# A gated linear recurrence and a spatial gating unit in one kernel: from scheduled batches to a hand-ordered pipeline of chunks

## The chip, the cores and the metric

The kernel runs on one core of a Trainium2 chip. The metric is device time in microseconds (us). A core has TensorE (PE in the profile; PEld is its weight loading), VectorE (DVE), ScalarE (ACT), GpSimd (POOL) and SyncE (SP), which take their instructions in order, each from its own queue, and signal each other by semaphores. Sixteen DMA engines move data between HBM and SBUF; TensorE writes into the eight banks of PSUM.

## The reference

Batch 4, 8 heads, sequence 768, head dimension 48; model width 384, d_ff 1024. The inputs and the output are float32.

```python
# part 1, for every batch and head
for t in range(S):
    state = alpha[t][:, None] * state + outer(k[t], v[t])
    y[t] = q[t] @ state
# part 2, x is y as (batch, seq, heads * dim)
h = relu(x @ w_in);  u, v = h[..., :512], h[..., 512:]
v_n = (v - mean(v)) / sqrt(var(v) + 1e-6)          # over the last axis
v_s = einsum('ts,bsd->btd', w_spatial, v_n) + b_spatial[None, :, None]
out = (u * v_s) @ w_out
```

## The kernel before

Part 1 cuts the sequence of a batch into six chunks of 128 steps, with all eight heads of a chunk side by side (128 partitions, 384 columns). `part1_front` loads q, k and v with a cast to bf16 from GpSimd's queue (L137 to L139) and alpha in float32 from SP's (L140); takes the logarithm of alpha (`la`, L143), sums it along time with a matmul by a triangle of ones (`cum_ps`, L146), and takes both exponentials (L151, L152). q is multiplied by the one on VectorE (`qt`, L158), k by the other on GpSimd (`kt`, L159). Sixteen small matmuls give each head's k^T v and its total decay (L164, L170), from which the state is carried on (L175 to L183: ScalarE, VectorE, GpSimd, ScalarE). q and k are transposed on TensorE (L190, L191), copied into `qkT` by VectorE for the even heads (L193) and by ScalarE for the odd ones (L194), and multiplied head by head (L202); VectorE applies the causal mask (`ptm`, L209). `part1_back` adds the part inside the chunk and the part from the state (L222, L228), and transposes y into `xT_b` (L237 to L242).

Part 2 works on a whole batch: v from x and its statistics (L264 to L274), the normalisation (L276 to L279), u (L289, L295), the mix along the sequence as eight groups of one bias matmul and six others (L300, L306) with the product by u on VectorE (`gT`, L312), and the output (L322 to L330), whose DMA is issued by ScalarE.

The text of the kernel puts part 1 of the next batch in front of part 2 of this one. The order on each engine is not that of the text: a scheduling pass of the framework chooses it, and the trace shows instructions of both parts mixed. That pass, or the compiler behind it, also puts a table load (`ACT_TABLE_LOAD`) in front of a ScalarE function whose table isn't loaded: in the groups they stand under the line of the logarithm (L143, L276) or the exponential (L151, L175, L277). Weights are loaded once, by GpSimd, after the text of the first batch's part 1 (`load_weights`).

## Time and profile before

| | |
|---|---|
| times of the two runs | 263.28 and 271.05 us, median 267.16 us |
| span of the profiled execution | 269.6 us, 4324 instructions |
| its own time | not listed apart; of the two, only 271.05 is as long as its span |
| mean granted clock of TensorE | 0.829 of 2.4 GHz |
| moved by DMA | 19.15 MB, 105060 packets, 100304 of them under 512 B |

Busy time counts an instruction from its start to its end; matmuls are pipelined and overlap, so a busy TensorE is not one at its peak. Where an engine stood idle, the profile names what released it.

### The profile page before, as it was taken

To read this page: it belongs to the slowest core of one execution; us is meant where nothing else is said; L and a number is where in the kernel's file an instruction comes from. 1 tells how busy PE (TensorE), PEld (TensorE's weight loads), DVE (VectorE), ACT (ScalarE), POOL (GpSimd) and SP (SyncE) were. 2 spreads that over 40 slices of the span, in tenths; PEclk is the share of its full clock that TensorE was granted. 3 is DMA by queue.
4 is the path that set the end of the run, shared out by engine and by line. 5 is a ranking of instruction groups with operands and counts; after the bars stand their busy time and mean duration, and the time that the engine had idled before them with its cause. 6 is when DMAs were issued, how large, how long until landed. Compare 5 with 4: busy or idle time off the path is not lost.

```text
span 269.6 us, 4324 instructions
## 1 busy us (share of the span) xinstructions
PE 191.8 (71%) x1664; PEld 116.2 (43%) x1676; DVE 144.7 (54%) x294; ACT 161.9 (60%) x264; POOL 106.2 (39%) x126
## 2 busy tenths in 40 slices
PE   0234475567657599968574959996696799995993
PEld 0123353346445355535342634454464434542351
DVE  7423626564444779412693766624588754286330
ACT  5884999499979833259979752039965500291003
POOL 9669836689992448303772321101340000000000
PEclk9999999867955569986688575999687759997799
DMA  9999999999999458933996222022000000220004
GB/s 139 153 158 89 100 205 201 102 101 107 109 96 102 44 32 44 77 116 87 106 55 33 17 15 15 2 88 88 2 0 2 0 2 1 88 88 0 2 0 176
DMA packets 105060, 19.15 MB, mean 71 GB/s; under 512 B 100304, under 2 KB 104656, under 8 KB 105040
## 3 DMA queue, kind: packets, MB, share of 16 engines
q0 software_dynamic: 76624, 9.44, 55.7%
q1 hardware_dynamic: 24960, 4.72, 10.5%
q10 hardware_dynamic: 3456, 4.72, 4.7%
q8 instruction: 13, 0.21, 0.3%
q14 instruction: 7, 0.06, 0.1%
HBM read 23.60 MB, written 4.72 MB: 105 GB/s over the span
## 4 chain that ended last, share of the span: by engine, by line
PE 36%; ACT 23%; POOL 12%; DMA 10%; issue 9%; DVE 7%; ACTq 1%; POOLq 0%; DVEq 0%
PE p2ps L306 14%; ACT L143 5%; PE p2ps L289 5%; PE p2ps L322 4%; PE p2ps L300 3%; POOL kt L159 3%; DMA vc<-in_v_dram 3%; POOL qc L137 3%; DMA w_in_sb<-in_moe_w_in_dram 3%; ACT qkT L194 3%; ACT la L143 3%; DMA kc<-in_k_dram 2%; POOL kc L138 2%; POOL s_state L181 2%; PE ptg L202 2%
## 5 line engine op out<-in xcount | busy, mean ns | idle before, releaser
L329 ACT COPY o_sb<-p2ps 128x384 f32<-128x384 f32 x24 | 11.0, 478 | 54.2 <-PE p2ps L322 48.7
L306 PE MATMUL p2ps<-w_spT,vn_sb 128*128 128x384 bf16 x192 | 41.2, 351 | 0.0
L209 DVE TENSOR_TENSOR ptm<-ptg,mask 128x512 bf16<-128x512 f32 x48 | 30.9, 685 | 15.3 <-PE ptg L202 14.9
L159 POOL TENSOR_TENSOR kt<-kc,binv 128x384 bf16<-128x384 bf16 x24 | 23.1, 964 | 38.6 <-PE ptr L191 12.6
L202 PE MATMUL ptg<-qkT 128*128 128x128 bf16 x192 | 24.5, 267 | 14.2 <-ACT qkT L194 10.4
L146 PE MATMUL cum_ps<-la,ut_ones 128*128 128x384 bf16 x24 | 10.6, 441 | 33.4 <-ACT la L143 27.9
L181 POOL TENSOR_TENSOR s_state<-s_state,bc_sb 48x384 f32<-48x384 f32 x16 | 14.5, 905 | 43.5 <-DVE s_state L180 43.5
L289 PE MATMUL p2ps<-xT_b,w_in_sb 128*128 128x384 bf16 x96 | 27.2, 424 | 5.0 <-DVE uT L295 3.4
L312 DVE TENSOR_TENSOR gT<-p2ps,uT 128x384 bf16<-128x384 f32 x32 | 17.8, 555 | 22.1 <-PE p2ps L306 22.1
L202 PEld LDWEIGHTS <-qkT 128*128 128x128 bf16 x192 | 16.8, 120 | 23.1 <-ACT qkT L194 14.8
L194 ACT COPY qkT<-ptr 64x1024 bf16<-64x1024 bf16 x24 | 24.2, 1009 | 3.9 <-DVE qkT L193 3.4
L139 POOL DMA_DIRECT2D vc<-in_v_dram x24 | 22.1, 921 | 11.1 <-PE y_ps L228 10.8
L237 ACT CAST x_sb<-y_ps 128x384 bf16<-128x384 f32 x24 | 11.5, 478 | 23.2 <-PE y_ps L228 23.2
L264 PE MATMUL p2ps<-w_in_sb,xT_b 128*128 128x512 bf16 x60 | 22.2, 456 | 3.1 <-issue 1.4
L306 PEld LDWEIGHTS <-vn_sb 128*128 128x128 bf16 x192 | 17.0, 103 | 15.4 <-issue 8.9
L138 POOL DMA_DIRECT2D kc<-in_k_dram x24 | 22.0, 918 | 2.1 <-POOL kt L159 2.1
L143 ACT ACT_TABLE_LOAD x17 | 21.8, 1283 | 1.0 <-PEq L358 0.7
L137 POOL DMA_DIRECT2D qc<-in_q_dram x24 | 22.0, 919 | 0.0
L193 DVE COPY qkT<-ptr 64x1024 bf16<-64x1024 bf16 x24 | 16.3, 679 | 10.6 <-PE ptr L191 10.5
L158 DVE TENSOR_TENSOR qt<-qc,b_exp 128x384 bf16<-128x384 bf16 x24 | 17.4, 726 | 8.5 <-DMA qc<-in_q_dram 6.4
L190 PE MATMUL ptr<-ident,qt 128*128 128x128 bf16 x96 | 18.2, 266 | 3.3 <-DVE ptm L209 3.3
L273 DVE BATCH_NORM_STATS2 stats<-v_sb 128x6 f32<-128x512 bf16 x24 | 16.0, 669 | 7.5 <-ACT v_sb L270 7.5
(62 smaller groups left out, 397.8 us busy)
## 6 DMA issues: line engine op xcount, KB each, us to landing
ac<-in_alpha_dram SPq DMA_DIRECT2D x24, 192.0 KB, 4.7
out_dram<-o_sb ACTq DMA_DIRECT2D x24, 192.0 KB, 1.8
qc<-in_q_dram POOLq DMA_DIRECT2D x24, 96.0 KB, 4.2
kc<-in_k_dram POOLq DMA_DIRECT2D x24, 96.0 KB, 4.2
vc<-in_v_dram POOLq DMA_DIRECT2D x24, 96.0 KB, 3.9
wsp_nat<-in_moe_w_spatial_dram POOLq DMA_DIRECT2D x1, 1152.0 KB, 12.2
w_in_sb<-in_moe_w_in_dram POOLq DMA_DIRECT2D x1, 768.0 KB, 8.2
w_out_sb<-in_moe_w_out_dram POOLq DMA_DIRECT2D x1, 384.0 KB, 9.1
```

The source lines that it names most:

```text
L137: nc.gpsimd.dma_start(out=qc, in_=q[b, :, t0:t0 + C, :].rearrange("h s d -> s h d"))
L138: nc.gpsimd.dma_start(out=kc, in_=k[b, :, t0:t0 + C, :].rearrange("h s d -> s h d"))
L139: nc.gpsimd.dma_start(out=vc, in_=v[b, :, t0:t0 + C, :].rearrange("h s d -> s h d"))
L143: nc.scalar.activation(out=la, in_=ac, func=AF.Ln)
L159: nc.gpsimd.tensor_mul(out=kt[:, :, :, 0:D], in0=kc_v, in1=bi_v)
L181: nc.gpsimd.tensor_tensor(out=s_state, in0=s_state, in1=bc_b, op=ALU.mult)
L194: nc.scalar.copy(out=qkT[0:64, 1::2, :, :], in_=trv_p[64:128, :, :, :])
L202: nc.tensor.matmul(out=ptf[:, j, :], lhsT=qkT[:, h, 1, :], rhs=qkT[:, h, 0, :], start=True, stop=True,)
L209: nc.vector.tensor_tensor(out=ptm, in0=ptf, in1=mask4, op=ALU.mult)
L264: nc.tensor.matmul(out=v_ps, lhsT=xT_b[:, ks, tt * 128:(tt + 1) * 128], rhs=w_in_sb[:, ks, DH:DFF], start=(ks == 0), stop=(ks == KS - 1),)
L289: nc.tensor.matmul(out=u_ps[:, 0:TH], lhsT=w_in_sb[:, ks, ft * 128:(ft + 1) * 128], rhs=xT_b[:, ks, th * TH:(th + 1) * TH], start=(ks == 0 ...
L306: nc.tensor.matmul(out=vs_ps[:, 0:TH], lhsT=vn_sb[:, st, dsl * 128:(dsl + 1) * 128], rhs=w_spT[:, st, th * TH:(th + 1) * TH], start=False, ...
```

## The change

Everything inside the kernel function is written anew; the matmuls of part 2 and the computation stay.

- Order: `manual_schedule()` keeps the order of the text on each engine. One loop runs over all 24 chunks of all batches. An iteration does the transposes of chunk i (`mid_tr`), the sums, exponentials and products of chunk i+1 (`front_cum`), the logarithm of chunk i+2 (`front_ln`), the head products, masks and state of chunk i (`mid_p`), its y (`back_y`) and the transposes of y (`back_xt`).
- Part 2 is cut into units in a queue, written as generators: after each matmul a unit yields a time in us, and `pump(us)` takes matmuls from the queue until that time is used up. Four calls per iteration take 0.8, 1.5, 0.8 and 0.4; after the last chunk the queue is emptied. A unit's evacuation is issued behind its last matmul.
- Loads: q, k, v and alpha all in float32 from SP's queue, four chunks ahead, seven buffers each; casting falls to the products and to GpSimd (`vb`). The outputs are issued from SP as well, 256 rows at a time. GpSimd loads w_in behind the products of chunk 0, the other weights in iteration 2; w_spatial is transposed after chunk 5.
- Heads stacked in pairs: two heads lie at partitions 0 to 47 and 64 to 111 of `qkT`, `kt` and the state; the state matmuls handle a pair at once (4 for 8, and 4 for the decays), the state's share of y 4 for 8. The head products use 48 rows each.
- ScalarE: one table set with logarithm and exponential is preloaded. The exponential for q is written back into PSUM. The relu of u moves here, over two PSUM banks at once; the cast of the state leaves for GpSimd.
- VectorE: masks of 512 columns as before; state adds in two halves; the copies of w_spatial's transposes; gT over two banks at once.

The added lines, cut (the removed ones are in the functions above):

```diff
+    io_pool = ctx.enter_context(tc.tile_pool(name="io", bufs=7))
...
+    pp_a = ctx.enter_context(tc.tile_pool(name="pp_a", bufs=2, space=bass.MemoryType.PSUM))
+    pp_p = ctx.enter_context(tc.tile_pool(name="pp_p", bufs=1, space=bass.MemoryType.PSUM))
+    pp_2 = ctx.enter_context(tc.tile_pool(name="pp_2", bufs=2, space=bass.MemoryType.PSUM))
+    ctx.enter_context(tc.manual_schedule())
+    nc.scalar.preload_act_table_set("natural_log_exp_and_others")
+    def load(i):
+        b, c = divmod(i, NCH)
+        t0 = c * C
+        tiles = {}
+        for name, src in (("ac", alpha), ("kc", k), ("qc", q), ("vc", v)):
+            t = io_pool.tile([128, H, D], FP32, name=name)
+            nc.sync.dma_start(out=t, in_=src[b, :, t0:t0 + C, :].rearrange("h s d -> s h d"))
+            tiles[name] = t
+        io[i] = tiles
+    load(0)
+    load(1)
...
+    queue = deque()
...
+    def unit_v(b, tt):
+        d = bt[b]
+        ps = pp_2.tile([128, 2, 512], FP32, name="ps2")
+        for ks in range(KS):
+            nc.tensor.matmul(
+                out=ps[:, 0, :], lhsT=d["xT"][:, ks, tt * 128:(tt + 1) * 128],
+                rhs=w_in_sb[:, ks, DH:DFF], start=(ks == 0), stop=(ks == KS - 1),
+            )
+            yield 0.225
+        nc.scalar.activation(out=d["v_sb"][:, tt, :], in_=ps[:, 0, :], func=AF.Relu)
+        stats = small.tile([128, 6], FP32, name="stats")
+        nc.vector.bn_stats(out=stats, in_=d["v_sb"][:, tt, :])
+        nc.vector.bn_aggr(out=d["mvs"][:, tt, :], in_=stats)
+        if tt == NT - 1:
+            nc.scalar.activation(out=d["rstd"], in_=d["mvs"][:, :, 1], func=AF.Ln, bias=eps_tile)
+            nc.scalar.activation(out=d["rstd"], in_=d["rstd"], func=AF.Exp, scale=-0.5)
...
+    def unit_u(b, fp, th):
...
+        nc.scalar.activation(
+            out=d["uT"][:, 2 * fp:2 * fp + 2, th * TH:(th + 1) * TH], in_=ps[:, :, 0:TH], func=AF.Relu)
+    def unit_s(b, dsl):
...
+        nc.vector.tensor_tensor(
+            out=d["gT"][:, dsl, :].rearrange("p (a t) -> p a t", a=2), in0=ps[:, :, 0:TH],
+            in1=d["uT"][:, dsl, :].rearrange("p (a t) -> p a t", a=2), op=ALU.mult,
+        )
+    def unit_o(b, tp):
...
+        o_sb = outp.tile([128, 2, DM], FP32, name="o_sb")
+        nc.scalar.copy(out=o_sb, in_=ps[:, :, 0:DM])
+        nc.sync.dma_start(
+            out=out[b, tp * 256:(tp + 1) * 256, :].rearrange("(j p) m -> p j m", p=128), in_=o_sb)
+    def pump(us):
+        while us > 0 and queue:
+            try:
+                us -= next(queue[0])
+            except StopIteration:
+                queue.popleft()
+    def front_ln(i):
+        la = la_bufs[i % NB]
+        nc.scalar.activation(
+            out=la[:, :, :, 0:D],
+            in_=io[i]["ac"].rearrange("p (hp s) d -> p hp s d", s=2), func=AF.Ln)
+    def front_cum(i):
+        st = P1[i] = {}
+        la = la_bufs[i % NB]
+        last = i % NCH == NCH - 1
+        cum = pp_a.tile([128, 512], FP32, name="cum", tag="a")
+        nc.tensor.matmul(out=cum[:, 0:DM], lhsT=ut_ones, rhs=la[:, :, :, 0:D], start=True, stop=True)
+        if not last:
+            for hp in range(HP):
+                nc.tensor.matmul(
+                    out=cum[:, DM + hp:DM + hp + 1], lhsT=la[:, hp, :, :], rhs=ones_col,
+                    start=True, stop=True)
+        cv = cum[:, 0:DM].rearrange("p (hp s d) -> p hp s d", hp=HP, s=2)
+        binv = work.tile([128, HP, 2, D], BF16, name="binv")
+        nc.scalar.activation(out=binv, in_=cv, func=AF.Exp, scale=-1.0)
+        if not last:
+            st["bc"] = small.tile([128, HP], FP32, name="bc")
+            nc.scalar.activation(out=st["bc"], in_=cum[:, DM:DM + HP], func=AF.Exp)
+        nc.scalar.activation(out=cv, in_=cv, func=AF.Exp)
+        t = io[i]
+        nc.gpsimd.tensor_mul(
+            out=kt_bufs[i % NB][:, :, :, 0:D],
+            in0=t["kc"].rearrange("p (hp s) d -> p hp s d", s=2), in1=binv)
+        nc.vector.tensor_mul(
+            out=qt_bufs[i % NB][:, :, :, 0:D],
+            in0=t["qc"].rearrange("p (hp s) d -> p hp s d", s=2), in1=cv)
+        st["vb"] = work.tile([128, H, D], BF16, name="vb")
+        nc.gpsimd.tensor_copy(out=st["vb"], in_=t["vc"])
+    def mid_tr(i):
+        st = P1[i]
+        pt = pp_p.tile([128, 2, HP, 128], FP32, name="pt")
+        qkT = work.tile([128, 2, HP, 128], BF16, name="qkT")
+        for j, src in enumerate((kt_bufs[i % NB], qt_bufs[i % NB])):
+            tr = pt[:, j].rearrange("p n t -> p (n t)").bitcast(BF16).rearrange("p (n t) -> p n t", n=8)
+            for hp in range(HP):
+                nc.tensor.transpose(tr[:, hp, :], src[:, hp, :, :], ident)
+            if j == 0:
+                nc.vector.tensor_copy(out=qkT[:, j], in_=tr[:, 0:HP, :])
+            else:
+                nc.scalar.copy(out=qkT[:, j], in_=tr[:, 0:HP, :])
+        st["qkT"], st["pt"] = qkT, pt
+    def mid_p(i):
+        st = P1[i]
+        qkT = st["qkT"]
+        c = i % NCH
+        pt = st["pt"]
+        for hp in range(HP):
+            for s in range(2):
+                nc.tensor.matmul(
+                    out=pt[:, s, hp, :], lhsT=qkT[64 * s:64 * s + D, 0, hp, :],
+                    rhs=qkT[64 * s:64 * s + D, 1, hp, :], start=True, stop=True)
+        ptm = work.tile([128, 2, HP, 128], BF16, name="ptm")
+        for s in range(2):
+            nc.vector.tensor_tensor(out=ptm[:, s], in0=pt[:, s], in1=mask4, op=ALU.mult)
+        st["ptm"] = ptm
+        if c == NCH - 1:
+            return
+        tp = pp_a.tile([128, HP, 2 * D], FP32, name="tp", tag="a")
+        for hp in range(HP):
+            nc.tensor.matmul(
+                out=tp[:, hp, :], lhsT=kt_bufs[i % NB][:, hp, :, :],
+                rhs=st["vb"][:, 2 * hp:2 * hp + 2, :].rearrange("p s d -> p (s d)"), start=True, stop=True)
+        ns = work.tile([128, HP, D], FP32, name="state")
+        bcb = st["bc"][:, :, None].to_broadcast([128, HP, D])
+        for s in range(2):
+            ps, pd = slice(64 * s, 64 * s + 64), slice(D * s, D * s + D)
+            if c == 0:
+                nc.vector.tensor_copy(out=ns[ps], in_=tp[ps, :, pd])
+            else:
+                nc.vector.tensor_tensor(out=ns[ps], in0=tp[ps, :, pd], in1=P1[i - 1]["state"][ps], op=ALU.add)
+        nc.gpsimd.tensor_tensor(out=ns, in0=ns, in1=bcb, op=ALU.mult)
+        sbd = sbd_bufs[i % NB]
+        nc.gpsimd.tensor_copy(out=sbd[0:64, :, 0:D], in_=ns[0:64])
+        nc.gpsimd.tensor_copy(out=sbd[64:128, :, D:2 * D], in_=ns[64:128])
+        st["state"], st["sbd"] = ns, sbd
+    def back_y(i):
+        st = P1[i]
+        c = i % NCH
+        y = pp_a.tile([128, H, D], FP32, name="y", tag="a")
+        n, tot = 0, H + (HP if c else 0)
+        if c:
+            sbd = P1[i - 1]["sbd"]
+            for hp in range(HP):
+                nc.tensor.matmul(
+                    out=y[:, 2 * hp:2 * hp + 2, :].rearrange("p s d -> p (s d)"),
+                    lhsT=st["qkT"][:, 1, hp, :], rhs=sbd[:, hp, :],
+                    start=(n == 0), stop=False)
+                n += 1
+        for h in range(H):
+            nc.tensor.matmul(
+                out=y[:, h, :], lhsT=st["ptm"][:, h % 2, h // 2, :], rhs=st["vb"][:, h, :],
+                start=(n == 0), stop=(n == tot - 1))
+            n += 1
+        x_sb = work.tile([128, KS, 128], BF16, name="x_sb")
+        nc.scalar.copy(out=x_sb, in_=y.rearrange("p h d -> p (h d)").rearrange("p (k t) -> p k t", k=KS))
+        st["x_sb"], st["y"] = x_sb, y
+    def back_xt(i):
+        st = P1.get(i)
+        b, c = divmod(i, NCH)
+        xv = st["y"].rearrange("p h d -> p (h d)").bitcast(BF16)[:, 0:KS * 128].rearrange(
+            "p (ks t) -> p ks t", ks=KS)
+        for ks in range(KS):
+            nc.tensor.transpose(xv[:, ks, :], st["x_sb"][:, ks, :], ident)
+        nc.vector.tensor_copy(out=bt[b]["xT"][:, :, c * C:(c + 1) * C], in_=xv)
+        queue.append(unit_v(b, c))
+        if c == 2 or c == NCH - 1:
+            for fp in range(NDS // 2):
+                queue.append(unit_u(b, fp, c // 3))
+        if c == NCH - 1:
+            for dsl in range(NDS):
+                queue.append(unit_s(b, dsl))
+            for tp in range(NT // 2):
+                queue.append(unit_o(b, tp))
+    def spatial_weights():
         for st in range(NT):
...
+            ps = pp_2.tile([128, 2, 512], FP32, name="ps2")
+            trv = ps[:, 0, :].bitcast(BF16).rearrange("p (n t) -> p n t", n=8)
             for tt in range(NT):
                 nc.tensor.transpose(trv[:, tt, :], wsp_nat[:, tt, st * 128:(st + 1) * 128], ident)
...
+            nc.vector.tensor_copy(out=w_spT[:, st, :], in_=trv[:, 0:NT, :].rearrange("p n t -> p (n t)"))
+    load(2)
+    front_ln(0)
+    front_cum(0)
+    nc.gpsimd.dma_start(out=w_in_sb, in_=moe_w_in.rearrange("(ks p) f -> p ks f", p=128))
+    load(3)
+    front_ln(1)
+    for i in range(N):
+        b, c = divmod(i, NCH)
         if c == 0:
...
+            batch_tiles(b)
+        if i + 4 < N:
+            load(i + 4)
+        mid_tr(i)
+        if i + 1 < N:
+            front_cum(i + 1)
+        if i == 2:
+            nc.gpsimd.dma_start(out=wsp_nat, in_=moe_w_spatial.rearrange("(tt p) s -> p tt s", p=128))
+            nc.gpsimd.dma_start(out=w_out_sb, in_=moe_w_out.rearrange("(ds p) m -> p ds m", p=128))
+            nc.gpsimd.dma_start(out=b_sp_sb, in_=moe_b_spatial[None, :])
+        pump(0.8)
+        if i + 2 < N:
+            front_ln(i + 2)
+        mid_p(i)
+        pump(1.5)
+        back_y(i)
+        pump(0.8)
+        back_xt(i)
+        pump(0.4)
+        if i == 5:
+            spatial_weights()
+    pump(1e9)
```

## Rows read from the trace of the kernel before

**Rows 1.** The page: engine busy times; granted clock of 40 equal slices.

```profile
PE 191.8 (71%) x1664; PEld 116.2 (43%) x1676; DVE 144.7 (54%) x294; ACT 161.9 (60%) x264; POOL 106.2 (39%) x126
...
PEclk9999999867955569986688575999687759997799
```

**Rows 2.** The page: chain of work that ended last, its shares by engine.

```profile
PE 36%; ACT 23%; POOL 12%; DMA 10%; issue 9%; DVE 7%; ACTq 1%; POOLq 0%; DVEq 0%
```

**Rows 3.** Waits: engine line <- releaser: us in total, times, longest us.

```profile
PE cum_ps L146 <- ACT la L143: 27.9, 17, 4.1
```

**Rows 4.** Windows, 182 to 198 us: stretch, busy (count), granted clock, DMA.

```profile
182.00:188.00 6.00, 4.32 (x61) 2.75 (x59) 2.48 (x5) 5.58 (x10) 0.82 (x1) 1.00 0.26 98
188.00:191.00 3.00, 0.94 (x21) 0.56 (x18) 1.95 (x3) 2.97 (x6) 2.01 (x2) 1.00 0.00 0
191.00:198.00 7.00, 6.09 (x63) 4.46 (x65) 4.52 (x9) 6.92 (x13) 2.40 (x2) 0.52 0.01 2
```

**Rows 5.** Groups by line, ScalarE: shapes, count, busy us, mean ns, idle before.

```profile
L194 ACT COPY qkT<-ptr 64x1024 bf16<-64x1024 bf16 x24 | 24.2, 1009 | 3.9 <-DVE qkT L193 3.4
...
L143 ACT ACT_TABLE_LOAD x17 | 21.8, 1283 | 1.0 <-PEq L358 0.7
...
L329 ACT COPY o_sb<-p2ps 128x384 f32<-128x384 f32 x24 | 11.0, 478 | 54.2 <-PE p2ps L322 48.7 <-DMA out_dram<-o_sb 5.0 <-ACT o_sb L329 0.5
...
L183 ACT CAST s_bf<-s_state 48x384 bf16<-48x384 f32 x20 | 10.2, 509 | 8.6 <-POOL s_state L181 7.2 <-DVE s_state L178 0.9 <-ACT o_sb L329 0.5
...
L277 ACT ACT_TABLE_LOAD x3 | 3.8, 1283 | 0.1
```

**Rows 6.** Groups by line, VectorE.

```profile
L209 DVE TENSOR_TENSOR ptm<-ptg,mask 128x512 bf16<-128x512 f32 x48 | 30.9, 685 | 15.3 <-PE ptg L202 14.9
...
L312 DVE TENSOR_TENSOR gT<-p2ps,uT 128x384 bf16<-128x384 f32 x32 | 17.8, 555 | 22.1 <-PE p2ps L306 22.1
L158 DVE TENSOR_TENSOR qt<-qc,b_exp 128x384 bf16<-128x384 bf16 x24 | 17.4, 726 | 8.5 <-DMA qc<-in_q_dram 6.4 <-PE ptr L190 2.0
...
L295 DVE TENSOR_SCALAR uT<-p2ps 128x384 bf16<-128x384 f32 x32 | 16.9, 547 | 4.7 <-PE p2ps L289 4.6
...
L193 DVE COPY qkT<-ptr 64x1024 bf16<-64x1024 bf16 x24 | 16.3, 679 | 10.6 <-PE ptr L191 10.5
...
L180 DVE TENSOR_TENSOR s_state<-s_state,t_ps 48x384 f32<-48x384 f32 x16 | 8.7, 541 | 13.8 <-ACT bc_sb L175 9.3 <-ACT s_bf L183 4.5
```

**Rows 7.** Groups by line, GpSimd.

```profile
L159 POOL TENSOR_TENSOR kt<-kc,binv 128x384 bf16<-128x384 bf16 x24 | 23.1, 964 | 38.6 <-PE ptr L191 12.6 <-ACT binv L152 9.7 <-issue 8.9
...
L137 POOL DMA_DIRECT2D qc<-in_q_dram x24 | 22.0, 919 | 0.0
```

**Rows 8.** Timeline, 200.4 to 201 us: start us, us, instruction.

```profile
200.49 0.22 PE L190 MATMUL ptr<-ident,qt 128*128 128x128 bf16 x1
...
200.88 0.22 PE L191 MATMUL ptr<-ident,kt 128*128 128x128 bf16 x1
```

**Rows 9.** Chain in order of time: start us, us, what.

```profile
177.57 3.90 PE p2ps L322 x24
...
243.62 2.03 DVE vn_sb L279 x6
...
248.68 2.03 PE p2ps L306 x6
...
258.64 1.08 PE p2ps L306 x6
```

**Rows 10.** Chain in order of time, 258 to 259 us.

```profile
258.38 0.26 PE p2ps L300
```

**Rows 11.** The page: the SP queue, its packets, MB and share of 16 engines.

```profile
q1 hardware_dynamic: 24960, 4.72, 10.5%
```

**Rows 12.** Windows: the first alpha load, and the weights' arrival.

```profile
2.50:3.50 1.00, 0.00 (x0) 0.00 (x0) 0.83 (x4) 0.03 (x1) 0.99 (x2) 1.00 1.09 218
34.00:48.00 14.00, 9.80 (x107) 6.59 (x109) 6.37 (x13) 13.06 (x22) 7.15 (x9) 1.00 1.25 201
```

More of the change, by code (lines that the diff above doesn't have):

```diff
@@ L2 @@
+from collections import deque
 from contextlib import ExitStack
@@ new lines @@
+    for i in range(NB):
+        la_i = consts.tile([128, HP, 2, 64], BF16, name=f"la{i}")
+        qt_i = consts.tile([128, HP, 2, 64], BF16, name=f"qt{i}")
+        kt_i = consts.tile([128, HP, 2, 64], BF16, name=f"kt{i}")
+        sbd_i = consts.tile([128, HP, 2 * D], BF16, name=f"sbd{i}")
+        nc.vector.memset(la_i, 0.0)
+        nc.vector.memset(qt_i, 0.0)
+        nc.vector.memset(kt_i, 0.0)
+        nc.vector.memset(sbd_i, 0.0)
+        la_bufs.append(la_i)
+        qt_bufs.append(qt_i)
+        kt_bufs.append(kt_i)
+        sbd_bufs.append(sbd_i)
@@ new lines, in unit_v @@
+    def unit_v(b, tt):
[14 more added lines that the diff above has]
+            nc.scalar.activation(out=d["rstd"], in_=d["rstd"], func=AF.Exp, scale=-0.5)
+            for t in range(NT):
+                nc.vector.tensor_scalar(
+                    out=d["vn"][:, t, :], in0=d["v_sb"][:, t, :],
+                    scalar1=d["mvs"][:, t, 0:1], scalar2=d["rstd"][:, t:t + 1],
+                    op0=ALU.subtract, op1=ALU.mult,
+                )
@@ new lines, in unit_u @@
+    def unit_u(b, fp, th):
+        d = bt[b]
+        ps = pp_2.tile([128, 2, 512], FP32, name="ps2")
+        for j in range(2):
+            ft = 2 * fp + j
+            for ks in range(KS):
+                nc.tensor.matmul(
+                    out=ps[:, j, 0:TH], lhsT=w_in_sb[:, ks, ft * 128:(ft + 1) * 128],
+                    rhs=d["xT"][:, ks, th * TH:(th + 1) * TH],
+                    start=(ks == 0), stop=(ks == KS - 1),
+                )
+                yield 0.17
+        nc.scalar.activation(
+            out=d["uT"][:, 2 * fp:2 * fp + 2, th * TH:(th + 1) * TH], in_=ps[:, :, 0:TH], func=AF.Relu)
@@ new lines, in unit_s @@
+    def unit_s(b, dsl):
+        d = bt[b]
+        ps = pp_2.tile([128, 2, 512], FP32, name="ps2")
+        for th in range(2):
+            nc.tensor.matmul(
+                out=ps[:, th, 0:TH], lhsT=ones_row, rhs=b_sp_sb[:, th * TH:(th + 1) * TH],
+                start=True, stop=False,
+            )
+            yield 0.17
+            for st in range(NT):
+                nc.tensor.matmul(
+                    out=ps[:, th, 0:TH], lhsT=d["vn"][:, st, dsl * 128:(dsl + 1) * 128],
+                    rhs=w_spT[:, st, th * TH:(th + 1) * TH],
+                    start=False, stop=(st == NT - 1),
+                )
+                yield 0.17
+        nc.vector.tensor_tensor(
+            out=d["gT"][:, dsl, :].rearrange("p (a t) -> p a t", a=2), in0=ps[:, :, 0:TH],
+            in1=d["uT"][:, dsl, :].rearrange("p (a t) -> p a t", a=2), op=ALU.mult,
+        )
@@ new lines, in unit_o @@
+    def unit_o(b, tp):
+        d = bt[b]
+        ps = pp_2.tile([128, 2, 512], FP32, name="ps2")
+        for j in range(2):
+            tt = 2 * tp + j
+            for dsl in range(NDS):
+                nc.tensor.matmul(
+                    out=ps[:, j, 0:DM], lhsT=d["gT"][:, dsl, tt * 128:(tt + 1) * 128],
+                    rhs=w_out_sb[:, dsl, :], start=(dsl == 0), stop=(dsl == NDS - 1),
+                )
+                yield 0.17
+        o_sb = outp.tile([128, 2, DM], FP32, name="o_sb")
+        nc.scalar.copy(out=o_sb, in_=ps[:, :, 0:DM])
+        nc.sync.dma_start(
+            out=out[b, tp * 256:(tp + 1) * 256, :].rearrange("(j p) m -> p j m", p=128), in_=o_sb)
```

269 lines of the change are left out of this document (30 added, 239 removed).

## The prediction

> **What bounds the kernel now.** I read the page's engine totals first [rows 1]: no engine is busy for much over 70% of the 269.6 us, and TensorE's 191.8 us is partly a matter of its clock, for the clock line stands at half speed (digit 5) or between in many slices after the first quarter. So no single engine is the bound; the order of the work is. The chain of waits says the same [rows 2]: the last-ending chain runs over TensorE 36%, ScalarE 23%, GpSimd 12%, DMA 10%, and 9% in which nothing visible was waited for. A typical link is the cumulative-sum matmul waiting for the logarithm (17 times, up to 4.1 us) [rows 3], and in front of that logarithm stands a table load. Last I looked at what the waits do to the clock [rows 4]: TensorE keeps the full clock (2.4 GHz level) while busy for 4.32 of 6 us, is then busy for 0.94 of 3 us, and the next 7 us are granted 0.52, near the 1.2 GHz level. Waiting costs twice.
>
> The run that was profiled: the span of 269.6 fits only the slower of the two times, 271.05, so some 1.45 us lie around it. The two differ by 3%; below 2% nothing of this kernel can be told from no change. My sum is built from durations, not scaled from the old span, so I compare it with the median as it is.
>
> **ScalarE.** 42 table loads in five groups (the first and the last stand in [rows 5]) of 1.283 us are 53.9 us; one is left. The transposed copy of 64x1024 at 1.009 us becomes one 128x512: between the 0.478 of 384 columns and 1.009, by the line 0.58; 24 times that saves 10. The state cast (10.2) goes to GpSimd. The relu of u comes over, 16 times 128x768, by the same line 0.80 each: 12.8. Output copies become 12 of 0.80 for 24 of 0.478: -1.4. Sum: 161.9-53.9+1.3-10.2-10.2+12.8-1.4 = 100 us, 4.2 per chunk. The row shows a 384-column copy out of PSUM at 0.478 on ScalarE [rows 5] and the relu at 0.547 on VectorE [rows 6], so the move is no loss in itself. The Trainium skill (ScalarE: Activation LUTs, Rules for kernel authors) says relu belongs on VectorE, up to about 3x faster there; by that the moved relus would cost some 50 us (an estimate from that page), 1.6 more per chunk; the rows contradict it for this source.
>
> **GpSimd.** 72 load issues of 0.92 us (three lines like the one row) go: -66 us [rows 7]. New are 24 casts of v and 40 half-size state casts; no row has them. Between nothing and the 0.964 of the two-input product at that size I take 0.9 and 0.5: +42, so 82 us, 3.4 per chunk, in the shade of everything else.
>
> **VectorE** [rows 6]. Out: relu of u 16.9. The copy 64x1024 (0.679) becomes 128x512; half the columns cost between 0.34 and 0.68, I take 0.41: -6.5. The q product read two SBUF operands at 0.726; with one in PSUM I take gT's 0.555: -4.1. gT becomes 16 of 768 columns, 0.95: -2.5. The state add (0.541) becomes two of half the columns, 0.34 each, 40 in all: +2.7 after the old 10.9. Six spatial copies: +3.3. Sum 121 us, 5.0 per chunk.
>
> **TensorE.** At full clock transposes follow each other 0.056 apart (eight from 200.49 to 200.88) [rows 8]. A chunk has 19 such matmuls of 128 columns (1.06), one of 384 (0.16, from 24 in 3.90 [rows 9]) and 20 of 96, 48 or 1 column, not dearer than 0.056 (1.1) nor cheaper than nothing: 1.2 to 2.4 us. Part 2 keeps its matmuls: 32 groups of 1.34 (0.26 [rows 10] + 1.08 [rows 9]), 4 times 3.90, 96 of 0.1625 and 72 of 0.217 (scaled by columns) are 90 us, 3.7 per chunk. Together 5.0 to 6.1.
>
> One thing speaks against the stacking. A group's one-row bias matmul makes seven matmuls take 1.34 where seven at 0.1625 take 1.14: 0.20 too much [rows 9, 10]. The 48-row products at partitions 0 and 64 may cost the same once a chunk, so TensorE stands at 5.2 to 6.3. The Trainium skill (TensorEngine Tiling (Array Packing), Key Properties) gives the reason: a change of tiling mode drains the array; the rows agree with it, and if every such drain lay on the path, the sum would be 3.6 us longer.
>
> **DMA.** A load of 197 KB on the SP queue takes between 1.18 us (10.5% of the span for 24 [rows 11]) and 0.90 (218 GB/s, with the first load under way [rows 12]). 96 of them are 86 to 113 us, 3.6 to 4.7 per chunk, outputs on the same queue beside them: not the bound in the steady part. The output DMAs wait for ScalarE's copy in SP's order, and loads queue behind them, but these are four chunks ahead.
>
> **The chunk's chain** sets the period, because each engine now takes its work in the written order. Links: eight transposes, 0.45 and 0.16 to finish; copy of q^T 0.58; two exponentials of 0.48 and a short one, 1.16; the q product of the next chunk 0.555, which VectorE has in front of the masks; two masks 1.37 [rows 6]; twelve matmuls 0.83 with the finish; copy of y 0.48; three transposes 0.33: 5.9 us, and with the last 0.4 of filler 6.2 from one chunk to the next. This is the added wait: the masks, and behind them y, queue on VectorE behind a product that waits for three ScalarE instructions. Part 2's instructions lie in the same queues, some 1.8 per chunk on VectorE and 1.5 on ScalarE (the sums above less the recurrence's own 3.2 and 2.7). Between none of them and half falls into the chain, 0 to 1.7, for half is issued where the engine has nothing of the chain to do; I take 0.3, nearer to none: P = 6.5.
>
> **The start.** Chunk 0 begins its transposes at about 7 (the first load and the same links). Chunks of the first batch have little filler, so 6.2 each, some 6.6 at half clock: 7+6x6.6 = 46.6, and the spatial transposes, whose six copies of 0.55 make 3.3: 50. By DMA: up to the alpha of chunk 6 25 loads are 22 to 30 us, the weights 2.36 MB at 201 GB/s [rows 12] 11.7, the first latency 2.5: 37 to 44; then 8.2 for logarithm, the rest of chunk 5 and the spatial copies: 45 to 52. TensorE also waits there for w_in, issued only behind chunk 0's products on GpSimd, with all of chunk 1 queued behind it. I take 50.
>
> **The end.** Filler is 3.5 us per chunk by the pump's own figures, 21 per batch against 21.7 of work, so 2.2 are left over; then the last v 0.65, u 1.95, the six normalisations (2.03 [rows 9]) and about as much for the relu and statistics before them, less the 2 that u hides, 2, eight groups of 1.34 10.7, a product 0.95, output 3.9, copy 0.8, landing 2.5: 26.
>
> **Sum.** 50 + 18x6.5 (117) + 26 = 193, with 1.45 around it 195.
>
> **Rivals.** (a) The queues absorb each other and TensorE is the bound at 5.8, DMA and clock not holding up the start (7+6x6.0+3.3 = 46): 46+104+24+1.5 = 176. For it: VectorE and ScalarE have less than 5.1 each. (b) Part 2's evacuations fall into the chain, P = 7.9: 52+142+27+1.5 = 222. For it: strict order, and only two PSUM buffers for filler and two for sums, states and y. (c) The change doesn't do what it says: the alternation of logarithm and exponential still loads tables, one of 1.28 in the chain: P = 7.8, and 3 at the start: 3+50+140+26+1.5 = 221. (d) Slower than before: TensorE's pauses in the chain keep its clock at the lower level. Six matmuls then take 2.03 for 1.08 [rows 9], 1.88 times; 6.1 becomes P = 11.4, the tail 40: 52+205+40+1.5 = 299. It decides against the change from P = 10.2, that is with three quarters of the pipeline at half clock. Against it: the chain leaves TensorE pauses of under 1 us, and the clock stayed at the full level from 182 to 188 us, where TensorE paused as well, and fell only behind the 3 us in which it hardly ran [rows 4].
>
> **Chances.** The forecast (P from 6.1 to 7.2) 0.45; (a) 0.2; (b) 0.22; (c) 0.06; (d) 0.04; the rest 0.03. (a) to (c) are all faster by over 2%, so faster 0.94; same 0.02; slower 0.04. The range runs from (a) to (b), 175 to 223.
>
> **What would show it.** One table load on ScalarE; load issues gone from GpSimd; masks that begin right after the q product of the next chunk; a period of 6.5 us between chunks from the second batch on, 50 us in; granted clock near full from there; a tail of 26 us with eight groups of 1.34. The prediction is wrong if the steady chunks wait for loads, if filler matmuls wait for a PSUM buffer, or if the clock line stays at 5.

## The result, and the profile after

The changed kernel took 238.75 us (median of 2 runs, 238.39 to 239.11) against 267.16. The two medians stand at 0.894; the ratio on record is 0.901 (95% interval 0.877 to 0.926). It is faster by a tenth, and 44 us slower than the forecast of 195, outside its range of 175 to 223. Some executions of a kernel show a lower granted clock and take 2 to 3% longer than the others (experiment 10: 197.3 and 198.8 us at 0.962 and 0.945, against 192.8 and 194.3 at 0.973), so where a kernel had both kinds, the shorter ones are compared.

The page of the changed kernel: span, TensorE's busy time, its granted clock and the SP queue.

```profile
span 236.6 us, 3858 instructions
...
PE 167.9 (71%) x1436; PEld 94.3 (40%) x1436; DVE 121.7 (51%) x270; ACT 94.9 (40%) x201; POOL 61.1 (26%) x121
...
PEclk9999999965557999999959999999799999977999
...
q1 hardware_dynamic: 103104, 23.60, 46.7%
```

Against [rows 1, 11]: ScalarE went from 161.9 to 94.9 us, VectorE from 144.7 to 121.7, GpSimd from 106.2 to 61.1, and the packets of the SP queue take 46.7% of the span for 10.5%. The clock line has one long dip, slices 9 to 13 (47 to 77 us), and short ones behind the batches (slice 21 above all), where before it was low in many slices. It says 9 from the first slice on, but up to 38 us the matmuls ran at half that pace (last section). TensorE is still busy for just 71%: there is room that the forecast had filled.

Groups by line of the changed kernel: shapes, count, busy us, mean ns of one, idle time before.

```profile
L190 DVE TENSOR_TENSOR gT<-ps,uT 128x768 bf16<-128x768 f32 x16 | 15.3, 954 | 7.5 <-PE ps L184 7.3
...
L266 ACT COPY qkT<-pt 128x512 bf16<-128x512 bf16 x24 | 14.1, 586 | 68.2 <-PE pt L262 68.2
L249 DVE TENSOR_TENSOR qt<-qc,cum 128x384 bf16<-128x384 f32 x24 | 13.3, 554 | 49.8 <-ACT cum L244 49.8
L171 ACT ACTIVATE uT<-ps 128x768 bf16<-128x768 f32 x16 | 12.7, 805 | 2.2 <-PE ps L165 2.2
...
L59 ACT ACT_TABLE_LOAD x1 | 1.3, 1283 | 0.7 <-PEq L398 0.7
```

One table load is left of 42 [rows 5]. The forecast's element times hold to a few ns (0.95, 0.58, 0.555, 0.80 in its text), so the error isn't in what instructions cost. It is in what waits for what. The waits of TensorE, the five largest (us in total, times, longest us):

```profile
PE pt L262 <- DVE qkT L264: 15.4, 24, 1.7
PE y L318 <- DVE ptm L281: 12.3, 17, 1.8
PE y L332 <- ACT x_sb L323: 9.4, 9, 4.8
PE ps L140 <- DVE xT L333: 7.2, 9, 1.3
PE ps L201 <- DVE gT L190: 4.3, 4, 1.3
```

The wait of [rows 3], cum for la, shrank from 27.9 us to 4.3, once. First now is one that comes in every chunk. One chunk's first lines in the timeline, at full clock (start us, us, instruction, idle time before it):

```profile
127.82 0.39 PE L262 MATMUL pt<-ident,kt 128*128 128x128 bf16 x4
...
128.24 0.42 DVE L264 COPY qkT<-pt 128x512 bf16<-128x512 bf16 x1 [0.49 <-PE pt L262]
...
128.72 0.38 PE L262 MATMUL pt<-ident,qt 128*128 128x128 bf16 x4 [0.52 <-DVE qkT L264]
```

The four transposes of q start only when VectorE has copied those of k: 0.90 us from first to first, where the forecast had all eight in 0.45. They write another PSUM bank, but of the same tile.

At a batch's end part 2's normalisation lies in front of the masks. VectorE's timeline there, with a ScalarE and a TensorE line that hang on it:

```profile
120.65 0.56 DVE L249 TENSOR_TENSOR qt<-qc,cum 128x384 bf16<-128x384 f32 x1 [2.26 <-ACT cum L244]
...
121.16 0.69 DVE L147 BATCH_NORM_STATS2 stats<-v_sb 128x6 f32<-128x512 bf16 x1
...
122.10 0.30 ACT L150 ACTIVATE rstd<-mvs,eps_tile 128x6 f32<-128x6 f32 x1 [0.98 <-DVE mvs L148]
...
122.68 2.03 DVE L153 TENSOR_SCALAR vn<-v_sb,mvs,rstd 128x512 bf16<-128x512 bf16 x6 [0.61 <-ACT rstd L151]
...
124.62 1.28 DVE L281 TENSOR_TENSOR ptm<-pt,mask 128x512 bf16<-128x512 f32 x2
...
125.36 0.20 PE L318 MATMUL y<-vb,ptm 128*128 128x48 bf16 x1 [0.40 <-DVE ptm L281]
```

The products that the masks need were done at 121.7; the masks start at 124.62.

**The period** below is the time from one copy of k (L264, 24 of them) to the next. From chunk 6 on it averages 7.89 us (17 intervals, 70.40 to 204.51) where the forecast had 6.5; inside a batch it runs 10.27, 7.02, 6.61, 7.53, 7.53, 8.61; the interval of 6.61 is called the quiet one below. The interval of 10.27, behind a batch's end, also paid in clock (us, then busy us and count of TensorE, its weight loads, VectorE, ScalarE, GpSimd; granted clock, DMA share, GB/s):

```profile
117.97:128.24 10.27, 8.96 (x58) 4.47 (x58) 6.00 (x15) 4.93 (x11) 2.54 (x5) 0.67 1.04 204
```

Chunk 6 starts its transposes at 69.7 us (forecast 50).

### The profile page after: what moved, and what is told of

It reads as the page before. It is cut to its first block, busy times and chain, and to the rows that moved or that the text cites. A ratio compares the mean times of both kernels' runs of the same rounds, so it can differ in the third digit from the quotient of the medians.

```text
span 236.6 us, 3858 instructions
## 1 busy us (share of the span) xinstructions
PE 167.9 (71%) x1436; PEld 94.3 (40%) x1436; DVE 121.7 (51%) x270; ACT 94.9 (40%) x201; POOL 61.1 (26%) x121
## 3 DMA queue, kind: packets, MB, share of 16 engines
q1 hardware_dynamic: 103104, 23.60, 46.7%
## 5 line engine op out<-in xcount | busy, mean ns | idle before, releaser
L246 POOL TENSOR_TENSOR kt<-kc,binv 128x384 bf16<-128x384 f32 x24 | 21.8, 910 | 90.8 <-issue 44.3
L266 ACT COPY qkT<-pt 128x512 bf16<-128x512 bf16 x24 | 14.1, 586 | 68.2 <-PE pt L262 68.2
L184 PE MATMUL ps<-w_spT,vn 128*128 128x384 bf16 x192 | 39.6, 326 | 0.0
L140 PE MATMUL ps<-w_in_sb,xT 128*128 128x512 bf16 x72 | 25.5, 453 | 9.8 <-DVE xT L333 7.2
L281 DVE TENSOR_TENSOR ptm<-pt,mask 128x512 bf16<-128x512 f32 x48 | 30.6, 678 | 1.7 <-PE pt L276 1.7
L165 PE MATMUL ps<-xT,w_in_sb 128*128 128x384 bf16 x96 | 24.2, 392 | 0.0
L201 PE MATMUL ps<-w_out_sb,gT 128*128 128x384 bf16 x96 | 18.9, 326 | 4.3 <-DVE gT L190 4.3
L184 PEld LDWEIGHTS <-vn 128*128 128x128 bf16 x192 | 15.7, 97 | 10.7 <-issue 3.8
L318 PE MATMUL y<-vb,ptm 128*128 128x48 bf16 x192 | 11.2, 192 | 12.3 <-DVE ptm L281 12.3
L190 DVE TENSOR_TENSOR gT<-ps,uT 128x768 bf16<-128x768 f32 x16 | 15.3, 954 | 7.5 <-PE ps L184 7.3
L264 DVE COPY qkT<-pt 128x512 bf16<-128x512 bf16 x24 | 10.1, 421 | 12.7 <-PE pt L262 12.7
L145 ACT ACTIVATE v_sb<-ps 128x512 bf16<-128x512 f32 x24 | 14.4, 599 | 3.7 <-PE ps L140 3.6
```

Source lines behind the costliest of these rows:

```text
L140: nc.tensor.matmul(out=ps[:, 0, :], lhsT=d["xT"][:, ks, tt * 128:(tt + 1) * 128], rhs=w_in_sb[:, ks, DH:DFF], start=(ks == 0), stop=(ks == ...
L145: nc.scalar.activation(out=d["v_sb"][:, tt, :], in_=ps[:, 0, :], func=AF.Relu)
L165: nc.tensor.matmul(out=ps[:, j, 0:TH], lhsT=w_in_sb[:, ks, ft * 128:(ft + 1) * 128], rhs=d["xT"][:, ks, th * TH:(th + 1) * TH], start=(ks ...
L184: nc.tensor.matmul(out=ps[:, th, 0:TH], lhsT=d["vn"][:, st, dsl * 128:(dsl + 1) * 128], rhs=w_spT[:, st, th * TH:(th + 1) * TH], start=Fal ...
L190: nc.vector.tensor_tensor(out=d["gT"][:, dsl, :].rearrange("p (a t) -> p a t", a=2), in0=ps[:, :, 0:TH], in1=d["uT"][:, dsl, :].rearrange( ...
L201: nc.tensor.matmul(out=ps[:, j, 0:DM], lhsT=d["gT"][:, dsl, tt * 128:(tt + 1) * 128], rhs=w_out_sb[:, dsl, :], start=(dsl == 0), stop=(dsl ...
```

## The experiments

Unless another is named, each is one edit to the changed kernel, against its 238.75 us. Theory A: the chunk's chain sets the period, longer by links that the forecast left out. B: TensorE's work at its clock does. C: part 2's two PSUM buffers do. A2 is A for part 2's instructions: they cost the chain wherever one of the chain stands behind them.

The kernel before took 265.9 to 270.1 us beside experiments 1 to 4, 262.8 to 268.0 beside 5 to 8 and 264.0 to 271.4 beside 9 to 11, and the changed kernel was not run again beside any. So differences of some 2 us between totals (3 and 4) show nothing by themselves; the intervals of the traces carry the argument.

**1. Two PSUM tiles for the transposes and products.**

```diff
-pt = pp_p.tile([128, 2, HP, 128], FP32, name="pt")
+pt = [pp_p.tile([128, HP, 128], FP32, name=f"pt{j}") for j in range(2)]
...
```

> One edit to the changed kernel: the two-bank PSUM tile of the transposes and products becomes two tiles of one bank each, so the transposes of q no longer wait for VectorE's copy of the transposed k. Theory A (the chunk's chain sets the period, and this wait of some 0.65 us is a link of it): the period of the quiet chunks falls from 6.6 to about 6.0, the wait of TensorE for that copy vanishes, and 24 times 0.4 to 0.65 us come off 238.4: 223 to 229 us. Theory B (TensorE's work at the clock it gets sets the period): the wait vanishes but comes back elsewhere; above 235. Theory C (part 2's two PSUM buffers set it): above 235, and the wait for the relu of u or for gT grows past 3 us from 2.

224.9 us (224.1 to 225.7): 13.9 off, as A had it. The wait for the copy of k is gone and the quiet interval fell from 6.61 to 5.66. Between the two traces 7.9 us lie in the 17 steady intervals and 2.5 in the start (first copy of k to that of chunk 6); another 2.1 lie in the end, which has no such wait and whose clock was 0.93 for 0.89. Windows of that interval, before and after the edit (columns as above):

```profile
135.26:141.87 6.61, 6.11 (x62) 3.50 (x62) 4.10 (x9) 2.43 (x6) 2.55 (x5) 1.00 0.00 0
```

```profile
130.00:135.66 5.66, 5.66 (x62) 3.23 (x60) 4.10 (x10) 2.36 (x6) 2.55 (x5) 1.00 0.00 0
```

In the second TensorE has no idle time left: where nothing waits, B's floor is reached. The Trainium skill (Perfetto Trace Analysis, Matmuls) says that independent matmul groups should rotate through different PSUM banks, so that one's evacuation overlaps the next's matmuls. The runs agree, and add that another bank of the same tile wasn't enough here.

**2. Part 2's VectorE instructions behind the masks.** Those of a chunk's first pump are kept back until mid_p is issued.

```diff
+holding[0] = True
 pump(0.8)
+holding[0] = False
 ...
 mid_p(i)
+flush()
```

> One edit to the changed kernel: the VectorE instructions of part 2 (statistics, normalisation, product with u) that the first pump of a chunk would put ahead of the two masks are issued behind the masks. Theory A (these instructions lie in the chunk's chain in front of the masks): the four periods of 7.5 us in a batch fall to about 6.6, the one of 10.3 behind a batch's end to about 8; 8 to 15 us off 238.4: 223 to 230 us. Theory B (TensorE's work at its clock): above 235. Theory C (part 2's two PSUM buffers): slower than 238, since the product with u now keeps its buffer longer, and TensorE's waits for gT grow.

234.4 us (234.3 to 234.4): 4.4 off, a miss for A's size. The 17 steady intervals still take 134.2 us (134.1 without the edit), those of 7.53 among them; what came off lies in the start and the end. In one chunk of a batch the output's first unit still drew a product with u ahead of the masks. The interval at a batch's end stayed at 10.2. Its timeline shows where the wait went:

```profile
120.97 0.69 DVE L149 BATCH_NORM_STATS2 stats<-v_sb 128x6 f32<-128x512 bf16 x1
...
121.92 0.30 ACT L152 ACTIVATE rstd<-mvs,eps_tile 128x6 f32<-128x6 f32 x1 [2.74 <-DVE mvs L150]
...
122.37 1.49 ACT L175 ACTIVATE uT<-ps 128x768 bf16<-128x768 f32 x2
...
123.21 0.32 PE L182 MATMUL ps<-b_sp_sb,ones_row 1*128 1x384 bf16 x1 [2.65 <-ACT uT L175]
...
123.46 0.37 PE L336 MATMUL y<-vb,ptm 128*128 128x48 bf16 x8
```

The masks were early, but the statistics now came late, the deviation waited for them on ScalarE, the relu of u stood behind the deviation, a matmul of part 2 waited for that relu's buffer, and y behind the matmul. One queue was mended and three others passed the wait on.

**3. The transposes of w_spatial as filler** from chunk 4, counted at 0.06 us each, in place of the block behind chunk 5.

> One edit to the changed kernel: the 36 transposes of w_spatial with their six copies, a block behind chunk 5 in which TensorE did nothing else from 61.4 to 69.7 us, enter the queue of filler at chunk 4 and run between the stages. Theory A (the block lies bare in the chain): the interval of 16.8 us at the first batch's end falls to about 10, so 230 to 233 us. Rival (the copies take VectorE's time in front of the masks of chunks 4 to 6 instead, or the units of the first batch are late and the work comes back at the end): above 236.

236.1 us (236.0 to 236.3): 2.6 off, less than A said. The start became 3.6 us shorter, but the interval behind the first batch rose from 10.27 to 11.83. A pump of 1.5 "us" took 25 transposes; they waited on two buffers for copies that VectorE had behind the masks, and y of chunk 4 came late:

```profile
51.92 2.14 PE L348 MATMUL ps<-ident,wsp_nat 128*128 128x128 bf16 x17 [1.92 <-DVE w_spT L350]
...
53.85 0.53 PE L312 MATMUL y<-sbd,qkT 128*128 128x96 bf16 x4
```

**4. The logarithm behind the copy of y.** front_ln(i + 2) moves behind back_y(i).

> One edit to the changed kernel: ScalarE's logarithm of chunk i+2 is issued behind the copy of y of chunk i and not ahead of the products, so that a late alpha holds up nothing behind it in ScalarE's queue. Theory A (the logarithm of chunk 2 waits 6.2 us for its alpha, and the copy of y of chunk 0 stands behind it): the second interval, 12.3 us, falls to about 8, and 233 to 235 us come out. Rival (the first chunks wait for the alpha in any case, one chunk later): the interval moves to the next chunk, 238 us. Slower, 240 or more, if the logarithm then comes too late for the cumulative sums of the steady chunks.

236.8 us (236.2 to 237.3): 2.0 off, half of A's least gain. The first interval (the expectation's second) fell from 12.27 to 9.96, but the one behind the first batch rose from 10.27 to 11.71.

**5. Experiment 1, with part 2's VectorE work placed by hand:** never between q's product and the masks; the deviation behind the copy of y; the normalisation behind the next copy of k, and the sums that need it wait in the queue until then.

```diff
 mid_tr(i)
+vnorm()
 ...
 back_y(i)
+norm()
```

> The two PSUM tiles of the first experiment, and part 2's VectorE instructions by hand: statistics and the product with u never between q's product and the masks (issued behind the masks), the reciprocal deviation on ScalarE only behind the copy of y, the six normalisations only behind the next copy of k, where VectorE stands idle for some 2 us in front of q's product. The second experiment had moved the normalisation behind the masks, but the deviation then stood in ScalarE's queue in front of the relu of u, and TensorE waited 2.65 us for that relu with y behind it. Theory A2 (part 2's instructions cost the chain wherever an instruction of the chain stands behind them; here none does): the interval behind a batch's end falls from 10.5 to about 8 and the quiet ones from 6.9 towards 6.2: 207 to 215 us. Rival (TensorE's work at its clock, the six matmul groups per chunk of some 5 us, is the floor by now): 220 to 225.

213.7 us (213.2 to 214.1): 11.2 less than experiment 1, inside A2's range. The traces have the same gain in the 17 steady intervals, 126.2 to 114.9. The interval behind a batch's end is now 5.79 (10.42 in experiment 1).

**6. All of it:** 5, the logarithm of 4, w_spatial's transposes counted at 0.2 us, and a chunk's matmuls fed behind its last pump.

> All edits together: the fifth kernel, and the logarithm behind the copy of y, a chunk's part-2 matmuls entering the queue only behind its last pump, and the transposes of w_spatial as filler that is counted at 0.2 us each (in the third experiment they were counted at 0.06, so that four units of six ran in one pump and their copies held y for 6 us). Theory A2: the start until chunk 6 falls from 68 to about 58, the intervals at a batch's end lose another 1 us each: 192 to 204 us, which is what the forecast's chain of 6.5 us would give. Rival (the floor is TensorE's work, or the first batch waits for its loads, of which the queue brings one chunk in 4 us): 207 or more.

200.7 us (200.0 to 201.4), 0.763 of the kernel before (0.752 to 0.774). Windows of the start (first copy of k to that of chunk 6) and the 17 steady intervals, in the changed kernel, experiment 1, 5 and 6:

```profile
7.10:70.40 63.30, 35.84 (x293) 21.69 (x293) 25.55 (x56) 18.97 (x43) 16.91 (x31) 0.84 1.04 195
70.40:204.51 134.11, 106.22 (x1000) 60.25 (x1000) 81.71 (x178) 64.35 (x139) 40.91 (x79) 0.95 0.38 86
```

```profile
7.00:67.76 60.76, 33.18 (x292) 21.02 (x295) 25.58 (x56) 18.83 (x43) 17.58 (x32) 0.76 1.04 195
67.76:193.93 126.17, 106.86 (x1003) 61.92 (x1006) 81.78 (x178) 65.23 (x141) 40.91 (x79) 0.92 0.42 96
```

```profile
7.03:62.94 55.91, 33.18 (x292) 21.18 (x295) 25.95 (x57) 18.83 (x43) 17.03 (x31) 0.88 1.06 193
62.94:177.87 114.93, 101.54 (x992) 59.10 (x996) 80.91 (x175) 62.80 (x138) 41.48 (x79) 0.97 0.51 113
```

```profile
7.02:50.02 43.00, 27.97 (x288) 18.81 (x290) 24.23 (x54) 18.57 (x42) 17.14 (x31) 0.84 1.08 197
50.02:164.64 114.62, 99.79 (x997) 58.34 (x1002) 81.45 (x176) 63.24 (x139) 41.62 (x79) 1.00 0.61 134
```

Per steady chunk: the changed kernel 7.89, TensorE busy 6.25 of it; experiment 6 6.74, busy 5.87 at full clock. Some 0.4 us of TensorE's time had been clock, lost with the waits; 1.64 us of idle time became 0.87. All that 6 gains on 5 lies in the start, where loads are now late: VectorE waits 4.55 us for the q of one chunk, while DMA moves 197 GB/s. C wasn't tried by itself; the changed kernel's waits for the relu of u's buffer are 2.0 us of L140 and 1.3 of L178.

**7. No table named at the start.**

```diff
-nc.scalar.preload_act_table_set("natural_log_exp_and_others")
```

> One edit to the changed kernel: no activation table is named at the start, so that logarithm and exponential load their own tables by turns. Theory A (the first exponential of a chunk stands in the chain behind the copy of q, so one load of 1.28 us does too, and the other one, in front of the logarithm, has ScalarE's idle time in which y is awaited): 24 times 1.3 to 2.0 us more, 270 to 287 us. Rival (ScalarE is 40% busy, the loads lie in idle time): under 245. If fewer than 24 loads show, the choice of tables was no problem in this order of instructions, and 238 to 250 come out.

292.2 us (292.2 and 298.7): more than A's most, and above the 262.8 to 268.0 of the kernel before beside it. Groups by line:

```profile
L222 ACT ACT_TABLE_LOAD x24 | 30.8, 1283 | 4.1 <-DMA ac<-in_alpha_dram 3.7
...
L239 ACT ACT_TABLE_LOAD x24 | 30.8, 1283 | 0.4
...
L149 ACT ACT_TABLE_LOAD x4 | 5.1, 1283 | 0.1
...
L150 ACT ACT_TABLE_LOAD x4 | 5.1, 1283 | 0.1
```

The quiet interval rose by 1.38 (6.61 to 7.99), one load, as A said: 33 us of 24 chunks. The other 24 lie in ScalarE's idle time in such a chunk, but elsewhere part 2's evacuations queue behind the loads (TensorE's wait of L177 for the relu of u went from 1.3 to 16.2 us), and the granted clock of the 17 intervals fell from 0.95 to 0.85.

**8. q, k and v cast by loads that GpSimd issues,** as before the change.

> One edit to the changed kernel: q, k and v come as before the change, cast to bf16 by loads that GpSimd issues (72 issues of 0.92 us), only alpha by SP. Theory A (GpSimd has 61 us of work in 237, the issues of a chunk, 2.8 us, stand in front of its k product, which waits for the exponential 2.5 us after the chunk's first transpose anyway): 236 to 243 us, so that this part of the change bought little in time. Rival (the issues or the casts delay the k product or the state, on which the next chunk's transposes and y wait): 0.5 to 2.8 us a chunk, 250 to 305 us.

247.6 us (247.56 to 247.60), between the two. In batch 2 the intervals are within 0.02 of the changed kernel's, as A has it; the 8.8 us are in the start (first copy of k at 12.64 for 7.10, first interval 14.91 for 12.27). TensorE waits there for GpSimd's own constants and for weights:

```profile
PE ps L141 <- DMA w_in_sb<-in_moe_w_in_dram: 7.4, 1, 7.4
PE cum L233 <- POOL ut_ones L81: 7.4, 1, 7.4
```

**9. The next chunk's q product behind the masks,** the forecast's "added wait" taken away.

```diff
 mid_p(i)
+front_q(i + 1)
...
```

> One edit to the changed kernel: the product of the next chunk's q is issued on VectorE behind the masks instead of ahead of them (the second exponential writes an SBUF tile of its own, so that the buffer of the sums is free for y without it). This takes away the wait that the forecast called the added one: masks behind a product that waits for three ScalarE instructions. Theory A2 (an instruction is a link of the chain where one of the chain stands behind it): the masks start when the products are done, 0.7 to 0.9 us earlier in each chunk: 6.6 becomes 5.8, and 217 to 224 us come out. Rival (TensorE's work at its clock, or part 2's instructions in front of the masks, which stay): above 232.

236.9 us (236.9 and 243.8, the profile being of the second): A2's 217 to 224 are missed. The quiet interval stayed at 6.61; one of 7.53 in each batch fell to 6.24. The masks were no longer late there, yet y didn't limit: TensorE had filler. In this trace two intervals of 7.02 became 10.25 and 10.69, at a low clock, 6.9 us that also lie between the two times:

```profile
130.13:140.38 10.25, 9.45 (x62) 4.81 (x62) 4.99 (x9) 2.31 (x6) 2.92 (x5) 0.61 0.01 2
```

**10. Experiment 6 with that late product.**

> The sixth kernel (all edits, 200.7 us) with the next chunk's q product behind the masks as well. Theory A2: 17 steady intervals of 6.74 fall by 0.6 to 0.8: 186 to 192 us; the first batch gains little, since it now waits for its loads (4.6 us for the q of one chunk). Rival (TensorE is now the floor: it is busy 155 us of 198, some 5.4 us per chunk and 25 at the end): 194 or more.

193.5 us (192.8 and 194.3 of four times), the best version: 0.73 of the kernel before beside it (264.0 to 267.3). A2's 186 to 192 is missed, and the rival's 194 just as narrowly, so the total decides little. The steady interval moved only from 6.74 to 6.62, and the quiet one stayed at 6.34, of which TensorE is busy for 6.34 in both. The rival holds for that quiet interval; over the 17, TensorE is busy for 99.0 of 112.6 us.

**11. A chunk's matmuls fed behind its last pump,** alone.

> One edit to the changed kernel: a chunk's part-2 matmuls enter the queue of filler behind the chunk's last pump, so that they never stand, waiting for the copy of x^T, in front of the next chunk's transposes. Theory A2 (waits of 0.5 to 1.3 us, nine of them, 7.2 us in all, and up to 0.8 us of matmuls behind each): 9 to 13 us less where the queue had run dry, 226 to 230 us. Rival (the work comes back in the next chunk's pumps, in front of the masks' products or y): above 235.

243.9 us (243.5 to 244.4): slower by 5, a miss in sign. The total hides two large effects, read from windows of the start and of the 17 steady intervals (63.30 and 134.11 us in the changed kernel):

```profile
6.90:58.37 51.47, 31.73 (x291) 19.89 (x291) 25.39 (x56) 19.25 (x43) 17.24 (x32) 0.87 1.07 197
58.37:212.06 153.69, 117.26 (x999) 64.52 (x999) 82.65 (x178) 63.44 (x139) 41.01 (x79) 0.89 0.41 90
```

The start became 11.8 us shorter: the waits for x^T fell from 7.2 to 1.4 us. The steady part became 19.6 longer: the normalisation now ended up in front of the masks with nothing of part 2 ahead of y, and the output matmuls reached a product with u that VectorE had behind the masks, with y behind them:

```profile
117.27 0.20 PE L318 MATMUL y<-vb,ptm 128*128 128x48 bf16 x1 [3.19 <-DVE ptm L281]
...
144.74 0.99 PE L201 MATMUL ps<-w_out_sb,gT 128*128 128x384 bf16 x5 [2.73 <-DVE gT L190]
...
145.57 0.33 PE L312 MATMUL y<-sbd,qkT 128*128 128x96 bf16 x4
```

**12. Experiment 6 without filler between the stages.**

> The sixth kernel (all edits but the late q product) with its pumps taken out: nothing of part 2 runs between the stages, all of it runs in a block behind the last chunk of each batch. The intervals inside a batch then show the chunk's chain by itself. The forecast's links, with the eight transposes as one step, make it 5.9 at full clock, and some 6.3 at the half clock that a bare chain may be granted. Theory A (the chain alone sets the period, filler lies in its gaps): 5.9 to 6.3, hardly less than the 6.74 with filler. Theory D (by now TensorE's own work, 5.8 us a chunk with filler, and its bare waits set it, and the chain is shorter): the intervals fall to 5 or less at full clock. The total is no guide here: 24 times that interval and four blocks of some 25 us, 230 to 260 us.

281.8 us, one run, slower than the 264.6 of the kernel before beside it; the intervals with part 2's block took 36 to 39 us, 30 to 33 more than a chunk, for the expected 25. Windows of one chunk of the first batch and three of the second:

```profile
28.06:33.88 5.82, 3.99 (x43) 2.97 (x42) 3.15 (x8) 2.42 (x6) 3.04 (x7) 1.00 1.12 188
...
88.07:93.89 5.82, 3.99 (x43) 2.98 (x42) 3.15 (x8) 2.42 (x6) 2.55 (x5) 0.50 1.11 219
93.89:99.71 5.82, 3.99 (x43) 2.97 (x42) 3.15 (x7) 2.42 (x6) 2.55 (x5) 0.50 0.90 178
99.71:105.53 5.82, 3.99 (x43) 2.97 (x42) 3.15 (x7) 2.42 (x6) 2.55 (x5) 0.50 1.13 223
```

The chain by itself takes 5.82 us, at half the clock (for the first row's 1.00 see the last section): just under A's bounds, above D's at a clock that D hadn't reckoned with, so neither is shown. With filler the clock is full, and there the chain is shorter: eight transposes take 0.62 us for 1.05 here, the three of y 0.33 for 0.50, the last seven products of y 0.35 for 0.46, which leaves some 5.1 (an estimate from these rows of experiments 6, 12 and the changed kernel). TensorE's own work, 5.87 a chunk at full clock in experiment 6, is then the longer of the two, and 6.6 to 6.7 is that work with the waits that are left in it.

## Why the prediction was wrong

The forecast's three terms, against both kernels (us; chunk 6's transposes start at 69.69 and 49.34; the end is the span less the other two):

| term | forecast | changed kernel | experiment 6 |
|---|---|---|---|
| start | 50 | 69.7 | 49.3 |
| 18 chunks | 18 x 6.5 = 117 | 18 x 7.89 = 142.0 | 18 x 6.74 = 121.3 |
| end | 26 | 24.9 | 27.7 |

**The step that failed is the chain's first link, "eight transposes, 0.45 and 0.16 to finish".** The code has two steps with VectorE's copy between them, since one tile holds both: 0.90 us from the first of k to the first of q. Undoing it is worth 13.9 us (experiment 1), 0.47 per steady chunk. A slip of 0.1 comes on top: 5.9 and the last 0.4 of filler are 6.3, not 6.2, 1.8 us over 18 chunks.

**"Between none and half falls into the chain; I take 0.3".** Its reason, that half is issued where the engine has nothing of the chain to do, was no evidence of position: the first pump puts part 2's instructions exactly between q's product and the masks. Moving them out, and the rest of their queues with them, took 11.2 us (5 against 1), 0.66 per steady chunk. With experiment 1's 0.47 that makes 1.13 of the 1.39 by which the period was off.

**The start, "6.2 each, some 6.6 at half clock ... and the spatial transposes, whose six copies make 3.3".** In the first batch filler stands in the way: a chunk's own matmuls wait for x^T and hold the next transposes (0.5 us and more), intervals were 8.0 to 8.9; the logarithm of chunk 2 waited 6.2 us for its alpha with the copy of y behind it; and the six rounds of w_spatial took 1.45 each, transposes and copy in turn at half clock, 8.2 us for 3.3. Experiment 6 took 13.0 us out of this (against 5), and then the forecast's bound by DMA, 45 to 52, was met at 49.3. Its three edits, made alone on the changed kernel, shortened the start by 3.6, 2.0 and, the late feed of experiment 11, 11.8 us. So, as far as these show, most of it was a chunk's filler in front of the next chunk's transposes; the totals of 2.6, 2.0 and -5 hide this. How the three add up in experiment 6 wasn't tried.

13.9, 11.2 and 13.0 are the steps from the changed kernel to experiment 6, 38 of the 44 us. The period of experiment 6, 0.24 over the forecast in 18 chunks, is most of what is left. That it comes so near to 6.5 is in part luck: the forecast's chain at full clock would be some 5.1 (experiment 12), and what fills the period is TensorE's work.

**What held.** Work per engine: ScalarE 94.9 for 100, VectorE 121.7 for 121, TensorE 5.87 per chunk inside 5.2 to 6.3; GpSimd 61.1 for 82, since the casts took 0.50 and 0.34 us. Moving the relu was no loss: 768 columns took 0.805 us on ScalarE, where two of 384 on VectorE took 1.09 [rows 6]. The Trainium skill (ScalarE: Activation LUTs, Rules for kernel authors) puts relu on VectorE, with a gain that it gives for bf16; for this source, float32 in PSUM, the times are against it. The end was right. So was the main gain: one table, without which the new order loses to the old kernel (experiment 7).

**The rivals.** (b), part 2's evacuations in the chain, named 7.9 and had 7.89 happen, though a third of the excess (0.47 of 1.39) was the shared tile; its 222 was low by the start. (a), 5.8, came true only in single intervals: 5.66 in the quiet one of experiment 1, where no wait was left. (c) is refuted by the single load. (d) holds for part of the interval behind a batch's end (0.67 there, 0.95 over the steady part), and for the chain without filler (0.50).

Experiments 9 and 10 correct the forecast's picture too: it took q's product in front of the masks for a fixed link, and removing it gave 0.12 us per chunk, for filler covers it. Theory A in its strict form fell there; what fits the runs, though no run isolates it, is TensorE's own work plus those waits that stand bare in its queue, and the clock that they cost.

## What to carry to other kernels

Where every engine takes its work in written order, price a hand-made pipeline by walking each queue and asking what stands in front of each instruction of the chain and what *that* waits for; engine totals and idle time can't tell it. Check which instructions share a tile, for it is the tile that is waited for. And try such moves together: three made alone gave 2.0 to 4.4 us and one lost 5, while moves of these kinds on all queues at once gave 24 (experiment 6 against 1). Read each by stages as well as by its total: the one that lost 5 had made the start 11.8 us shorter.
